# One-core attention and two feed-forward stages: SP's order of stores and loads in the second unit loop and at the start of the last stage

## The chip, the core and the metric

The kernel runs on one core of one Trainium2 chip. The metric is device time in microseconds (us) of the whole program. Three runs of the kernel before took 1477.15, 1477.49 and 1480.37 us; the median is 1477.49. Engines are named as in the profile: PE is TensorE, PEld its weight load, DVE VectorE, ACT ScalarE, POOL GpSimd, SP the engine whose queue issues nearly all DMAs.

## The reference

```python
def reference(**kwargs):                     # names cut
    attn_out = _attn_ref(q, k, v)            # keys and values mean-pooled by 8, softmax attention, 8 x 8 heads, 576 rows
    x = attn_out.transpose(0, 2, 1, 3).reshape(B * S, H * D)          # 4608 tokens x 512
    # stage 1: each token goes to one of 8 experts (argmax of gate logits + a bias by modality)
    #   h = max(x[mask] @ w1[e], 0);  out[mask] = gate_w * (h @ w2[e])          512 -> 1024 -> 512
    x = _moe_ref(x=x, **moe_kwargs)
    # stage 2, all tokens:  h = x @ w_in;  g = h * clip(h + 3, 0, 6) / 6;  g @ w_out   512 -> 2048 -> 512
    return _moe2_ref(x=x, **moe2_kwargs)
```

`w_in` and `w_out` come as float64, of which the kernel makes pairs of float32 (a high part and a rest).

## The kernel before, in words

Attention fills the first 210 us or so. Its end sorts the tokens by expert into a DRAM table `xr`, and a small table in SBUF (`tab`) says for each *unit* of 400 rows which expert it belongs to.

Stage 1 (`moe1`) works unit by unit (`unit`, L930). A unit has eight *steps* f, one per 128 hidden columns. In step f SP loads the weights of step f+3 into one of two buffers `ws`; ScalarE and VectorE split the weights of step f+2 into `wh` and `wl` (L783, L784); TensorE forms the hidden product `ph` (L942, 12 matmuls), then the output products `y` of step f-1 (L955, 12 matmuls). At the end of a unit the next unit's rows `cxg` are transposed (L868), where ScalarE also copies the token numbers out (`tkr`, L873), and `yo` takes the result, which the next unit stores to `yd`. There are one first unit, a loop of eight units (in each of which 1/8 of `w_in` is converted), a second loop whose count `n_l` is read from `nun` at run time (L1045), and a last unit.

The second loop (L1046, body at L1019 to L1031) converts three tiles of `w_out` in each pass. Each tile is loaded to `ds` (two buffers, L1306), goes through nine operations of ScalarE and VectorE (`f64_split`, L792 to L807) into `wv` (two buffers), and is stored to `vd` (L1031). The tiles are loaded in steps 0, 1 and 2. The operations stand in one list, from which each step takes four. The stores stand at the end of steps 3, 5 and 7.

Stage 2 (`moe2`) takes blocks of 768 tokens; each block is eight *quads* of seven products `hps` (L1118, six matmuls each, with operands `sq` loaded from `sd` into seven buffers, L1295), and in quad q the twelve groups of output products `ops` (L1108) of quad q-1 stand between them. In the first block VectorE and ScalarE also convert the rest of `w_out`, two operations at a time. The results go out by an indirect DMA whose row numbers are `tki`.

Each engine executes its own instructions in the order in which the Python code issues them (a manual schedule on PE, ACT, DVE and SP). An instruction that waits holds everything behind it on its engine. So where a store or a load stands among SP's instructions decides what its wait holds up.

```python
                cs[f] = g.wo_load(cd, f)                                  # L1021, steps 0, 1, 2
                if f > 0 and f % 2 == 1 and f // 2 in range(1, KD + 1):   # the store, steps 3, 5, 7
    nc.sync.dma_start(tkf, tok_d[0:NT].rearrange("(c p) -> p c", p=P))    # L1189
    while g.s_ahead < 7:
        g.s_load()
```

Of the kernel before, what the change touches and what calls it, by code (L numbers as in the profile page):

```python
# [8 lines left out]
F32 = mybir.dt.float32  # L9
F32R = mybir.dt.float32r  # L10
BF16 = mybir.dt.bfloat16
I32 = mybir.dt.int32
# [7 lines left out]
P = 128  # L20
# [4 lines left out]
NT = B * S  # L25
# [16 lines left out]
KD = 3  # L42
# [768 lines left out]
def moe1(tc, g, xr_d, tok_d, y_d, s_d, v_d, w1, w2, w_in):  # L811
    nc = tc.nc
# [109 lines left out]
    def conv_out(t):  # L922
        a, m, ex = (s.cv.tile([P, 4, P], I32, name=n, tag=n).rearrange("p k f -> p (k f)") for n in ("a", "m", "ex"))
        o = s.cv.tile([P, 2, DM], F32R, name="wv", tag="wv", bufs=2)
        return o, f64_split(nc, g, t[:, :, 1], t[:, :, 0], a, m, ex, o[:, 0], o[:, 1])
# [4 lines left out]
    def unit(i, first=False, last=False, tail=None, quad=None):  # L930
# [3 lines left out]
        cs = {}  # L934
# [15 lines left out]
        def y_mm(f):  # L950
            j = f % 4
            hi, lo = hh.pop(f)
            for d in range(4):
                for n, (a, b) in enumerate(((s.wh, hi), (s.wl, hi), (s.wh, lo))):
                    nc.tensor.matmul(yps[d], a[j][:, 1, d * P:(d + 1) * P], b, start=(f == 0 and n == 0), stop=(f == 7 and n == 2))  # L955

        lx = LX if first else 1
        parts = {LX: (0, 1, 2, 3)} if first else {1: (0,), 2: (1,), 3: (2,), 4: (3,)}
        ops = []
        for f in range(8):  # L960
            if first and f == 0:
                w_dma(e, 2)
            if f == lx and not last:
                en = reg(0, i + 1, E - 1)
            if f < 5 or not last:
                w_dma(e if f < 5 else en, (f + 3) % 8)
            if f == 0 and not first:
                col = reg(2, i, NT)
                if not last:
                    cc = quad  # L970
                    if quad is None:
                        cd = nc.values_load(g.tab[0:1, 3, bass.ds(i, 1)], engines=(ET.SP,), min_val=0, max_val=1)
            if f < 6 or not last:
                w_split((f + 2) % 8)
            h_mm(f)
            if f == lx and not last:
                rx = reg(1, i + 1, E * R - NW)
            if f in parts and not last:
                load_x(rx, parts[f])
            if f - 1 in parts and not last:  # L980
                gate_x(parts[f - 1])
            if f == 2:
                store_tok(0 if first else reg(2, i + 1, NT))
            if f == 3 and not first:
                store_y(col)
            if f == 7 and not last:
                for c in range(2):
                    transp(c, ps())
            if f > 0:
                y_mm(f - 1)  # L990
            if tail and next(tail, None):
                open3()
            if last:
                if f in (1, 2):
                    g.y_load(0, f - 1)
                if f == 3:
                    ops = g.y_ops(0)
                if f >= 3:
                    g.s_load()
                    for _ in range(3):  # L1000
                        if ops:
                            ops.pop(0)()
                if f >= 6:
                    g.wo_load(KD + NQ * (f - 6))
            elif quad is not None:
                if f == 0:
                    cs[0], cs[1] = conv_load(cc, 0), conv_load(cc, 1)
                if f == 1:
                    co, ops = conv(cs.pop(0))
                if f == 4:  # L1010
                    c1_, ops = conv(cs.pop(1))
                for _ in range(5):
                    if ops:
                        ops.pop(0)()
                if f == 4:
                    conv_store(co, cc, 0)
                if f == 7:
                    conv_store(c1_, cc, 1)
            elif not first:  # L1019
                if f < KD:  # L1020
                    cs[f] = g.wo_load(cd, f)  # L1021
                if 1 <= f <= KD:
                    co, o_ = conv_out(cs.pop(f - 1))
                    ops += o_
                    cs[8 + f] = co
                for _ in range(4):
                    if ops:
                        ops.pop(0)()
                if f > 0 and f % 2 == 1 and f // 2 in range(1, KD + 1):
                    n = f // 2  # L1030
                    nc.sync.dma_start(v_d[bass.ds(cd, 1), n - 1].rearrange("o p x -> p (o x)"),  # L1031
                                      cs.pop(8 + n).bitcast(F32).rearrange("p w f -> p (w f)"))
        if not last:
            for c in range(2, 4):
                transp(c, ps())
        y_mm(7)
        for d in range(4):
            (nc.scalar.copy if d % 2 else nc.vector.tensor_copy)(s.yo[:, d], yps[d])

    def run(tail):  # L1040
        open_ps()
        unit(0, first=True, tail=tail)
        with tc.For_i(0, NQ, 1, iteration_sync="reg_based") as i:
            unit(i + 1, quad=i)
        n_l = nc.values_load(g.nun, min_val=2, max_val=10)  # L1045
        with tc.For_i(0, n_l, 1, iteration_sync="reg_based") as i:  # L1046
            unit(i + NQ + 1)
        unit(n_l + NQ + 1, last=True)
        store_y(reg(2, n_l + NQ + 2, NT))
        es_p.close()  # L1050
        es_l.close()
        es_r.close()
# [3 lines left out]
    return c  # L1056


def moe2(tc, g, tok_d, v_d, out):


    nc = tc.nc
# [20 lines left out]
    def wo_get(f):  # L1083
        nc.sync.dma_start(wo[f].bitcast(F32).rearrange("p w f -> p (w f)"), v_d[f // NQ, f % NQ])

    tkf = c1.tile([P, NT // P], F32, name="tkf")
    tki = c1.tile([P, NT // P], I32, name="tki")
    pso = {}

    def put(j, t):  # L1090
# [95 lines left out]
        rest(6)  # L1186
        return [lambda fh=fh, th=th, t=t: o_group(j, q, fh, th, t, out_[fh, th]) for fh, th in ((0, 0), (1, 0), (1, 1), (0, 1)) for t in range(TC)]

    nc.sync.dma_start(tkf, tok_d[0:NT].rearrange("(c p) -> p c", p=P))  # L1189
    while g.s_ahead < 7:  # L1190
        g.s_load()
    wo_get(0)
# [3 lines left out]
    for n, f in enumerate(fs):  # L1196
        o_ = []
        cops += [lambda f=f, o_=o_: (o_.extend(conv(f)), o_.pop(0)())] + [lambda o_=o_: o_.pop(0)()] * 5
        if n + 2 < len(fs):
            cops.append(lambda f=fs[n + 2], o_=o_: (o_.pop(0)(), g.wo_load(f)))  # L1200
        cops += [lambda o_=o_: o_.pop(0)()] * (9 - len(cops) % 9 if len(cops) % 9 else 0)
    groups = []
    yo = []
    for j in range(NP):
        for q in range(NQ):
            extra = {i: [] for i in range(7)}
            if j == 0:
                for i in range(7):
                    for _ in range(2):
                        if cops:  # L1210
                            extra[i].append(cops.pop(0))
                if q == 1:
                    extra[0].append(lambda: v.tensor_copy(tki, tkf))
                if q < KD - 1:
                    extra[3].append(lambda q=q: wo_get(q + 1))
                    extra[4].append(lambda q=q: wo_get(NQ + q + 1))
# [24 lines left out]
def chunk_kernel(ctx, tc, q, k, v, mid, w_gate, mbias, w1, w2, w_in, w_out, out):  # L1241
# [9 lines left out]
    with tc.manual_schedule(engines={ET.PE, ET.Activation, ET.DVE, ET.SP}):  # L1251
# [5 lines left out]
            g.sp, g.yp = pool("ds"), pool("dy")  # L1257

        g.open_d = open_d
        g.raw, g.yc = {}, {}  # L1260
        g.sq, g.s_ahead = [], 0

# [49 lines left out]
        tail = attention(tc, g, c, (q, k, v, mid, w_gate, mbias), xr_d)  # L1312
        next(tail)
        c.run(tail)
        moe2(tc, g, tok_d, v_d, out)


# [28 lines left out]
```

## Time and profile before

| | |
|---|---|
| median of 3 runs | 1477.49 us (1477.15 to 1480.37) |
| profiled execution | 1480.39 us, span 1478.6 us |
| mean granted clock of PE | 0.973 |
| PE busy | 1400.0 us (95% of the span), 7673 matmuls |
| DVE busy | 948.0 us (64%) |
| ACT busy | 622.8 us (42%) |
| passes of the second loop | 2 (six stores `vd<-wv`) |

All views are of one profiled execution. Times in a view are us from the start of the span. [...] A stretch's busy time counts what an engine did in it; its length less that is standing. Waits of SP's queue and of the engines are listed apart.

### The profile page before, as it was taken

To read this page: it belongs to the slowest core of one execution; us is meant where nothing else is said; L and a number is where in the kernel's file an instruction comes from. 1 tells how busy PE (TensorE), PEld (TensorE's weight loads), DVE (VectorE), ACT (ScalarE), POOL (GpSimd) and SP (SyncE) were. 2 spreads that over 40 slices of the span, in tenths; PEclk is the share of its full clock that TensorE was granted. 3 is DMA by queue.
4 is the path that set the end of the run, shared out by engine and by line. 5 is a ranking of instruction groups with operands and counts; after the bars stand their busy time and mean duration, and the time that the engine had idled before them with its cause. 6 is when DMAs were issued, how large, how long until landed. Compare 5 with 4: busy or idle time off the path is not lost.

```text
span 1478.6 us, 24692 instructions
## 1 busy us (share of the span) xinstructions
PE 1400.0 (95%) x7673; PEld 1282.2 (87%) x7673; DVE 948.0 (64%) x1920; ACT 622.8 (42%) x1255; POOL 204.1 (14%) x231
## 2 busy tenths in 40 slices
PE   7998988999999999878899999999999999999998
PEld 6787877999999998878788888888888888888886
DVE  7899774778887876656687544644554465465443
ACT  3565653445555543444344333433333343333322
POOL 5555233111111111000000100000010000001001
PEclk8999998999999999999899999999999999999999
DMA  9974154777777766656754454454355445435441
GB/s 267 312 227 167 73 163 126 247 233 245 240 238 244 241 217 203 202 178 182 266 171 143 149 162 117 117 174 139 116 154 163 116 124 179 125 115 155 116 118 67
DMA packets 236172, 258.40 MB, mean 175 GB/s; under 512 B 25442, under 2 KB 197474, under 8 KB 236082
## 3 DMA queue, kind: packets, MB, share of 16 engines
q1 hardware_dynamic: 228882, 237.08, 53.0%
q0 software_dynamic: 7200, 20.18, 3.7%
q8 instruction: 49, 0.80, 0.2%
q14 instruction: 41, 0.34, 0.1%
HBM read 209.36 MB, written 55.24 MB: 179 GB/s over the span
## 4 chain that ended last, share of the span: by engine, by line
issue 50%; PE 3%; POOL 2%; DMA 1%; DVE 0%; POOLq 0%; ACT 0%; SPq 0%; ACTq 0%
POOL out_dram L1097 2%; PE ph L942 1%; PE y L955 1%; DMA sq<-sd 1%; PE hps L1118 0%; POOLq L1341 0%; ACT r L1129 0%; DVE r L1130 0%; DVE c L1139 0%; DVE da L795 0%; DVE dm L797 0%; POOLq L1097 0%; DVE gl L1134 0%; SPq L1189 0%; DVE dex L796 0%
## 5 line engine op out<-in xcount | busy, mean ns | idle before, releaser
L1118 PE MATMUL hps<-yc,sq 128*128 128x384 f32 x2004 | 411.9, 340 | 14.7 <-DVE c L1139 7.3
L1118 PEld LDWEIGHTS hps<-yc,sq 128*128 128x128 f32 x2004 | 362.8, 189 | 51.6 <-DVE c L1139 13.0
L1108 PE MATMUL ops<-wo,gh 128*128 128x512 f32 x1152 | 362.3, 395 | 0.0
L1108 PEld LDWEIGHTS ops<-wo,gh 128*128 128x128 f32 x1152 | 212.9, 188 | 23.0
L1108 PE MATMUL ops<-wo,gl 128*128 128x512 f32 x576 | 228.4, 397 | 0.0
L1129 ACT ACTIVATE r<-c,three 128x384 f32<-128x384 f32 x144 | 88.8, 617 | 225.9 <-DVE c L1139 225.5
L784 DVE TENSOR_TENSOR wl<-ws,wh 128x512 fp32r<-128x512 f32 x192 | 131.7, 719 | 60.4 <-ACT wh L783 53.1
L783 ACT CAST wh<-ws 128x512 fp32r<-128x512 f32 x192 | 115.0, 619 | 92.5 <-DMA ws<-in_moe_w_dram 67.7
L1133 ACT CAST gh<-r 128x384 fp32r<-128x384 f32 x192 | 98.6, 513 | 123.5 <-DVE r L1130 122.8
L1097 POOL DMA_INDIRECT out_dram<-osb,tki x36 | 35.3, 981 | 804.9 <-ACT osb L1095 774.5
L942 PE MATMUL ph<-xhi,wh 128*128 128x400 f32 x384 | 133.6, 348 | 7.1 <-issue 3.4
L955 PE MATMUL y<-hi,wh 128*128 128x400 f32 x384 | 136.6, 356 | 2.6 <-ACT hi L946 2.5
L955 PE MATMUL y<-lo,wh 128*128 128x400 f32 x384 | 135.3, 352 | 1.8 <-DVE lo L947 1.8
L942 PE MATMUL ph<-xlo,wh 128*128 128x400 f32 x384 | 134.2, 349 | 0.0
L955 PE MATMUL y<-hi,wl 128*128 128x400 f32 x384 | 133.9, 349 | 0.0
L942 PE MATMUL ph<-xhi,wl 128*128 128x400 f32 x384 | 133.9, 349 | 0.0
L1108 PEld LDWEIGHTS ops<-wo,gl 128*128 128x128 f32 x576 | 108.0, 188 | 26.3
L1134 DVE TENSOR_TENSOR gl<-r,gh 128x384 fp32r<-128x384 f32 x192 | 106.4, 554 | 27.0 <-ACT gh L1133 23.2
L1130 DVE SCALAR_TENSOR_TENSOR r<-r,c 128x384 f32<-128x384 f32 x144 | 80.4, 558 | 57.7 <-ACT r L1129 55.8
L860 POOL TENSOR_TENSOR cxg<-cxg 100x512 f32<-100x512 f32 x48 | 57.7, 1206 | 355.5 <-PE ph L942 178.1
L1129 ACT ACTIVATE r<-hps,three 128x384 f32<-128x384 f32 x48 | 27.9, 581 | 136.7 <-PE hps L1118 136.6
L1130 DVE SCALAR_TENSOR_TENSOR r<-r,hps 128x384 f32<-128x384 f32 x48 | 26.6, 553 | 90.2 <-ACT r L1129 90.1
(231 smaller groups left out, 1979.8 us busy)
## 6 DMA issues: line engine op xcount, KB each, us to landing
sq<-sd SPq DMA_DIRECT2D x336, 256.0 KB, 2.8
ws<-in_moe_w_dram SPq DMA_DIRECT2D x192, 256.0 KB, 3.8
sd<-wq SPq DMA_DIRECT2D x16, 896.0 KB
cxg<-xr SPq DMA_DIRECT2D x44, 225.8 KB
yd<-yo SPq DMA_DIRECT2D x12, 800.0 KB, 6.5
yr<-yd SPq DMA_DIRECT2D x12, 768.0 KB, 4.3
kv<-in_k_dram SPq DMA_DIRECT2D x16, 512.0 KB, 7.5
kv<-in_v_dram SPq DMA_DIRECT2D x16, 512.0 KB, 9.8
```

Of the source, the lines that this page charges most:

```text
L783: nc.scalar.copy(hi, src)
L784: nc.vector.tensor_tensor(lo, src, hi.bitcast(F32), op=ALU.subtract)
L860: nc.gpsimd.tensor_tensor(s.xg[:, t, 0:DM].rearrange("p (h x) -> p h x", x=D), v, s.xg[:, t, GC:GC + 1].unsqueeze(2).to_broadcast([T4, H, ...
L942: nc.tensor.matmul(ph, a[j][:, 0, k * P:(k + 1) * P], b[k], start=(n == 0), stop=(n == 11))
L955: nc.tensor.matmul(yps[d], a[j][:, 1, d * P:(d + 1) * P], b, start=(f == 0 and n == 0), stop=(f == 7 and n == 2))
L1097: i_ = nc.gpsimd.indirect_dma_start(out=out, out_offset=bass.IndirectOffsetOnAxis(ap=tki[:, c:c + 1], axis=0), in_=o, in_offset=None).ins
L1108: nc.tensor.matmul(pso[t_], gt[a][:, t * P:(t + 1) * P], wo[f][:, b], start=(q == 0 and fh == th and n == 0), stop=(q == NQ - 1 and fh != ...
L1118: nc.tensor.matmul(ps, w[:, kk, a * P:(a + 1) * P], y[:, b, kk], start=(start and n == 0), stop=(n == 5), skip_group_check=True)
L1129: a_.activation(r, c, AF.Relu, bias=g.three)
L1130: v.scalar_tensor_tensor(r, r, 6.0, c, op0=ALU.min, op1=ALU.mult)
L1133: a_.copy(gh, r)
L1134: late.append(lambda: v.tensor_tensor(gl, r, gh.bitcast(F32), op=ALU.subtract))
```

## The change

In the second loop a tile is loaded in steps 0, 1 and 4, its operations are taken five a step from steps 1, 3 and 5 on, and it is stored in steps 4, 6 and after the last products. The last unit loads one `sq` tile in each step from step 1 on (before: from step 3 on), loads the token numbers in step 3 as 36 rows of 128, and in step 7 transposes them on PE and casts them to `tki` on DVE. The read of the loop count stands before the first loop. In stage 2 the load of the conversion after next stands seven operations later.

```diff
+        def v_store(t, k):
+            nc.sync.dma_start(v_d[bass.ds(cd, 1), k].rearrange("o p x -> p (o x)"), t.bitcast(F32).rearrange("p w f -> p (w f)"))
...
+                if f == 3:
+                    nc.sync.dma_start(g.tk, tok_d[0:NT].rearrange("(c p) -> c p", p=P))
+                if f == 7:
+                    pt = ps()
+                    nc.tensor.transpose(pt[:, 0:NT // P], g.tk, g.idn[0:NT // P, 0:NT // P])
+                    nc.vector.tensor_copy(g.tki, pt[:, 0:NT // P])
+                if f >= 1:
+                    g.s_load()
                 if f >= 3:
-                    g.s_load()
...
             elif not first:
-                if f < KD:
-                    cs[f] = g.wo_load(cd, f)
-                if 1 <= f <= KD:
-                    co, o_ = conv_out(cs.pop(f - 1))
+                if f in (0, 1, 4):
+                    k = min(f, KD - 1)
+                    cs[k] = g.wo_load(cd, k)
+                if f in (1, 3, 5):
+                    cs[8 + f // 2], o_ = conv_out(cs.pop(f // 2))
                     ops += o_
-                    cs[8 + f] = co
-                for _ in range(4):
+                for _ in range(5):
                     if ops:
                         ops.pop(0)()
-                if f > 0 and f % 2 == 1 and f // 2 in range(1, KD + 1):
-                    n = f // 2
-                    nc.sync.dma_start(v_d[bass.ds(cd, 1), n - 1].rearrange("o p x -> p (o x)"),
-                                      cs.pop(8 + n).bitcast(F32).rearrange("p w f -> p (w f)"))
+                if f in (4, 6):
+                    v_store(cs.pop(8 + f // 2 - 2), f // 2 - 2)
...
         y_mm(7)
+        if 10 in cs:
+            v_store(cs.pop(10), 2)
...
         unit(0, first=True, tail=tail)
+        n_l = nc.values_load(g.nun, min_val=2, max_val=10)
         with tc.For_i(0, NQ, 1, iteration_sync="reg_based") as i:
             unit(i + 1, quad=i)
-        n_l = nc.values_load(g.nun, min_val=2, max_val=10)
...
-    nc.sync.dma_start(tkf, tok_d[0:NT].rearrange("(c p) -> p c", p=P))
...
-        if n + 2 < len(fs):
-            cops.append(lambda f=fs[n + 2], o_=o_: (o_.pop(0)(), g.wo_load(f)))
-        cops += [lambda o_=o_: o_.pop(0)()] * (9 - len(cops) % 9 if len(cops) % 9 else 0)
+        cops += [lambda o_=o_: o_.pop(0)()] * 3
+    for n, f in enumerate(fs[2:]):
+        one = cops[9 * n + 13]
+        cops[9 * n + 13] = lambda f=f, one=one: (one(), g.wo_load(f))
```

SP in the second loop before, from the weight load of step 5 (`ws`, two DMAs each) over the store of the second tile (`vd<-wv`) to the weight load of step 6; ISA and REGISTER_ALU are register instructions:

```order
L879 ISA
L879 DMA ws_2139<-in_moe_w_dram 128x512
L1031 ISA
L1031 REGISTER_ALU
L1031 DMA vd<-wv 128x1024
L877 ISA
L877 DMA ws_2140<-in_moe_w_dram 128x4x128
L879 ISA
L879 DMA ws_2140<-in_moe_w_dram 128x512
```

The same place in the change, with steps 5 and 6 in a row:

```order
L879 ISA
L879 DMA ws_2141<-in_moe_w_dram 128x512
L877 ISA
L877 DMA ws_2142<-in_moe_w_dram 128x4x128
L879 ISA
L879 DMA ws_2142<-in_moe_w_dram 128x512
L958 ISA
L958 DMA vd<-wv 128x1024
```

The second tile's store has moved behind the weight load of step 6; that of the third stands behind the weight load of step 7, the body's last.

SP at the end of the last unit and the start of stage 2 before: the last store of `yd`, the token numbers, then operands `sq` and converted tiles `wo`:

```order
L896 REGISTER_ALU
L896 DMA yd<-yo 128x4x400
L1189 DMA tkf<-tokd 128x36x1
L1295 DMA sq<-sd 128x2x256 x2
L1084 DMA wo_4643<-vd 128x1024
L1084 DMA wo_4635<-vd 128x1024
L1295 DMA sq<-sd 128x2x256 x3
L1306 DMA ds<-in_moe_w_out_dram 128x1024
L1084 DMA wo_4642<-vd 128x1024
L1295 DMA sq<-sd 128x2x256
```

The same place in the change:

```order
L896 REGISTER_ALU
L896 DMA yd<-yo 128x4x400
L1094 DMA wo_4653<-vd 128x1024
L1094 DMA wo_4645<-vd 128x1024
L1304 DMA sq<-sd 128x2x256 x3
L1094 DMA wo_4652<-vd 128x1024
L1304 DMA sq<-sd 128x2x256
L1094 DMA wo_4644<-vd 128x1024
L1304 DMA sq<-sd 128x2x256 x2
L1315 DMA ds<-in_moe_w_out_dram 128x1024
```

The load of the token numbers and two `sq` loads are gone from here (they stand in the last unit), and the load `ds` has moved from ahead of the second pair of `wo` loads to behind it.

## Rows read from the trace of the kernel before

**Rows 1.** The page, part 1: busy time (share of the span) and instructions of each engine.

```profile
PE 1400.0 (95%) x7673; PEld 1282.2 (87%) x7673; DVE 948.0 (64%) x1920; ACT 622.8 (42%) x1255; POOL 204.1 (14%) x231
```

**Rows 2.** Waits of TensorE, 552 to 712 us: us in total, times, longest.

```profile
PE pt L868 <- ACT tkr L873: 7.6, 2, 5.4
PE hps L1118 <- DMA sq<-sd: 6.7, 2, 4.0
PE ph L942 <- issue: 3.4, 1, 3.4
PE ph L942 <- PEq L1341: 3.4, 1, 3.4
```

**Rows 3.** Stretches: length, busy of PE, PEld, DVE, ACT, POOL; PEclk, DMA share, GB/s.

```profile
256.43:297.01 40.58, 38.51 (x209) 37.55 (x210) 30.00 (x52) 18.72 (x35) 4.27 (x4) 0.97 0.77 237
333.74:370.18 36.44, 36.44 (x210) 36.34 (x210) 29.43 (x53) 19.11 (x35) 4.72 (x4) 1.00 0.80 243
557.07:560.48 3.41, 3.41 (x12) 3.38 (x11) 0.58 (x1) 0.57 (x2) 0.00 (x0) 0.50 0.52 153
556.16:605.53 49.37, 42.09 (x209) 39.32 (x210) 31.20 (x51) 18.58 (x36) 4.93 (x4) 0.90 0.59 185
605.53:648.49 42.96, 38.74 (x210) 36.94 (x209) 31.64 (x52) 19.37 (x37) 4.44 (x4) 0.97 0.66 212
651.90:688.42 36.52, 36.52 (x192) 36.51 (x193) 22.84 (x33) 16.63 (x28) 0.00 (x0) 0.95 0.62 203
688.42:704.91 16.49, 9.79 (x43) 8.70 (x42) 10.89 (x23) 6.88 (x13) 0.00 (x0) 0.76 0.81 206
704.91:710.67 5.76, 5.76 (x16) 5.18 (x17) 2.06 (x5) 1.35 (x3) 0.00 (x0) 0.50 1.05 393
```

**Rows 4.** Waits of SP's queue, 555 to 652 us.

```profile
SPq L1031 <- DVE wv L807: 31.4, 6, 9.9
...
SPq L1046 <- DMA vd<-wv: 1.8, 1, 1.8
```

**Rows 5.** Timeline, 588 to 604 us: start, us, engine, line, operation, [idle before].

```profile
589.46 0.35 SPq L1031 DMA_DIRECT2D vd<-wv  x1
...
597.65 1.29 DVE L784 TENSOR_TENSOR wl<-ws,wh 128x512 fp32r<-128x512 f32 x2 [3.00 <-issue]
```

**Rows 6.** Waits of all engines, 555 to 652 us.

```profile
ACT wh L783 <- DMA ws<-in_moe_w_dram: 21.1, 12, 3.7
...
ACT ex L792 <- DMA ds<-in_moe_w_out_dram: 2.6, 2, 1.4
```

**Rows 7.** Timeline, 684 to 722 us.

```profile
688.42 4.57 PE L1118 MATMUL hps<-yc,sq 128*128 128x384 f32 x24
...
689.63 0.45 SPq L1189 DMA_DIRECT2D tkf<-tokd  x1
...
690.13 5.80 SPq L1295 DMA_DIRECT2D sq<-sd  x2
...
694.19 0.55 DVE L1139 TENSOR_TENSOR ww<-s,hps 128x384 f32<-128x384 f32 x1
...
695.73 0.55 DVE L1139 TENSOR_TENSOR c<-ww,ops 128x384 f32<-128x384 f32 x1
...
698.00 2.26 PE L1118 MATMUL hps<-yc,sq 128*128 128x384 f32 x6 [3.96 <-DMA sq<-sd]
...
704.91 2.29 PE L1118 MATMUL hps<-yc,sq 128*128 128x384 f32 x6 [2.73 <-DMA sq<-sd]
```

**Rows 8.** DMA view, 684 to 712 us: packets and their sizes.

```profile
DMA packets 8412, 6.17 MB, mean 220 GB/s; under 512 B 4864, under 2 KB 7692, under 8 KB 8411
```

**Rows 9.** Line 1045, the loop count's read: ns min/median/max, starts.

```profile
L1045 PEldq TENSOR_LOAD <-nun x1: 491/491/491, 554.0 to 554.0; - x1
```

**Rows 10.** Waits of TensorE, 712 to 800 us.

```profile
PE hps L1118 <- DVE c L1139: 0.8, 1, 0.8
```

**Rows 11.** DMA view, 300 to 550 us: packets by queue.

```profile
q1 hardware_dynamic: 63088, 60.20, 77.8%
```

More of the change, by code (lines that the diff above doesn't have):

```diff
@@ L1056, in moe1, with moe2 @@
     return c
-def moe2(tc, g, tok_d, v_d, out):
+def moe2(tc, g, v_d, out):
     nc = tc.nc
@@ L1084, in wo_get @@
         nc.sync.dma_start(wo[f].bitcast(F32).rearrange("p w f -> p (w f)"), v_d[f // NQ, f % NQ])
-    tkf = c1.tile([P, NT // P], F32, name="tkf")
-    tki = c1.tile([P, NT // P], I32, name="tki")
+    tki = g.tki
     pso = {}
@@ L1211, in moe2 @@
                             extra[i].append(cops.pop(0))
-                if q == 1:
-                    extra[0].append(lambda: v.tensor_copy(tki, tkf))
                 if q < KD - 1:
@@ L1259, in chunk_kernel @@
         g.open_d = open_d
+        g.tk = g.cp.tile([NT // P, P], F32, name="tk")
+        g.tki = g.cp.tile([P, NT // P], I32, name="tki")
         g.raw, g.yc = {}, {}
@@ L1314, in chunk_kernel @@
         c.run(tail)
-        moe2(tc, g, tok_d, v_d, out)
+        moe2(tc, g, v_d, out)
 _INS = ["q", "k", "v", "moe_modality_id", "moe_w_gate", "moe_modality_bias", "moe_w1", "moe_w2", "moe2_w_in", "moe2_w_out"]
```

## The prediction

> **What bounds the kernel now.** I read the engine shares first, then the mean and waits of TensorE, then stretches cut at the first matmul of each unit. [...] The waits of TensorE between 552 and 712 us name the standing: 7.6 us for a transpose behind ScalarE's `tkr`, 6.7 us for `sq` loads, 3.4 us at each end of the second loop [rows 2]. That is the region that the diff edits.
>
> The stretches give the size [rows 3]. A pass of the first loop takes 36.44 us with TensorE busy throughout. The second loop runs two passes in this execution (the six stores `vd<-wv` are three a pass), and they take 49.37 and 42.96 us for the same 210 matmuls and transposes. So 12.9 and 6.5 us are lost inside them. VectorE does 31.64 us of work in the second pass against 29.43 in the first loop's pass: 2 us more, well below 36.4, so VectorE's load is not the reason. The queue of SP is: it waited 31.4 us for VectorE at L1031, the store of a converted tile [rows 4]. SP works in order, so the weight loads of the next steps stand behind that store. In the first pass the second store went out only at 589.46, when TensorE had reached the eighth step's products. ScalarE accordingly stood 21.1 us waiting for weights [rows 6]. VectorE's `wl` of the last step came at 597.65, after 3.00 us in which nothing that the profile shows held it [rows 5]. TensorE stood 5.4 us there.
>
> The third place is the start of the last stage. SP issues the token-number load (L1189) at 689.63, and the two `sq` issues behind it span 5.80 us [rows 7], where the load of the token numbers itself is 0.45. Of the 8412 packets in 684 to 712 us, 4864 are under 512 B [rows 8]: that load reads 4608 numbers of 4 B, one packet each. TensorE stood 3.96 and 2.73 us for `sq` in the first quad [rows 7], and its clock was 0.50 until 710.67 [rows 3].
>
> **The change, part by part.** All is counted against the profiled execution: 1480.39 us, span 1478.6. The median of the runs shown, 1477.49, is 2.9 us lower; I subtract the same sum from it.
>
> *Stores two steps later, third load in step 4, five operations a step.* The instructions stay the same: three loads, 27 operations, three stores a pass. A tile's nine operations now fill steps 1 and 2 (3 and 4, 5 and 6), and its store stands in step 4 (6, end), so it finds its data ready; the weight load behind it no longer waits. What bounds a pass then? The first loop has the same 24 splits and its own 22 operations, at most five a step, and runs without a gap. I take 36.44 plus 0.8 for the 2 us more of VectorE: 37.2, so 5.8 less in the second pass. Bounds: 36.4 if nothing is late (6.5 less); 40 if ScalarE, whose queue takes the third tile one step after its load, stands for it (3 less): the waits of that kind in rows are small, 2.6 us in two [rows 6].
>
> The first pass pays for first use. The first loop's own first pass took 40.58, 4.1 above the later ones [rows 3]. Here the half clock from 557.07 to 560.48, which follows the 3.43 us of standing at the entry, costs 1.7, and stays. I take 36.4 + 1.7 + 3.4 = 41.5, so 7.9 less. Bounds: 38.1 (11.2 less), and 46.4 if the 3.00 us stop of VectorE still reaches TensorE with its half clock behind it (3 less). Step 7 now has no conversion operations, so that stop meets a VectorE with less behind it; that is why I go near the first loop's row.
>
> *Exit.* At the end of the second loop all engines meet, and SP there waits 1.8 us for the last store to land [rows 4]. The third store now goes out as soon as step 6 is done and lands during step 7 and the last products. 1.8 less; bounds 0 and 2.3. The last unit ran a little at 0.50 [rows 3], behind that standing of 3.4: the mean clock of 0.95 over 36.52 us is 1.8 lost. With 1.6 of standing I count half of it: 0.9 less, bounds 0 and 1.7.
>
> *Loop count read earlier.* Each engine reads the count in about 0.5 us [rows 9]. Between the loops all engines have just met, so it is paid in full (0.5 less); ahead of the first loop TensorE still has products queued, so I count 0.2 more. Bounds 0 and 0.5 less.
>
> *Last unit.* Two `sq` loads come in steps 1 and 2, so all seven are issued before the stage ends; there SP's DMA queue is free enough (share 0.62 [rows 3]) that weights are not late. Token numbers come as 36 rows of 512 B, are transposed by one TensorE instruction and cast by VectorE in step 7: 0.1 more (a 100x100 transpose is 0.25, pipelined). If weights did slip, the 4.6 us that a step lasts (36.44 over eight) is the bound.
>
> *Start of the last stage.* The 4608 packets and the blocked issue go. Next late are VectorE's operations. The first 24 matmuls took 4.57 us at full clock, 0.19 each [rows 7], so the 42 of the quad need 8.0. The sixth product overwrites what `ww` (694.19, 0.55) reads, the seventh what `c` (695.73, 0.55) reads [rows 7]; so TensorE waits 0.7 and some 0.5, and the quad ends near 697.5: 9.1 us instead of 16.49, 7.4 less. The half clock over the 5.76 us behind it gives back 2.9. Against that stands VectorE's debt, since TensorE reaches the second quad while VectorE still has about 3 us of the first quad's operations: I count 1.2, and 0.7 for a chance of 0.4 that the small waits still cost 1.7 in clock. Sum: 8.4 less. Bounds: 4 (TensorE is only let go when VectorE is done, and half the clock loss stays) and 10.5.
>
> *The loads of the later conversions* leave SP seven operations later. SP waits at them before, but TensorE's longest wait between 712 and 800 us is 0.8, for VectorE [rows 10], so I count nothing. The `sq` loads that stood behind it were covered by seven buffers; the price, if the later load makes ScalarE wait in turn, is a wait of the same 0.8 kind a few times, 3 at most.
>
> Sum: 7.9 + 5.8 + 1.8 + 0.9 + 0.3 - 0.1 + 8.4 = 25.0 less. From 1480.39 that is 1455.4, from the median 1452.5. All bounds on the poor side add up to about 10 less (1467.5), on the good side to 32.7 less (1445).
>
> **The rivals.**
> *First use and VectorE take the place of the waits.* The first pass keeps its 5.4 us gap and the clock behind it, since the 3.00 us stop is no SP wait, and the last stage gets only its lower bound of 4. For it: that stop and the debt are in rows. Against: in the second pass the same place cost 2.2 with weights late, and VectorE is freer now. 3 + 5.8 + 1.8 + 0.3 + 4 = 14.9 less: 1462.6.
>
> *The second loop stays bound.* If ScalarE and VectorE hand tiles to each other too late even with weights on time, the passes keep 49 and 43, and only the exit and the last stage gain: 1.8 + 0.3 + 8.4 = 10.5 less, 1467. Against it stands the first loop's pass with nearly the same load.
>
> *Slower: code is fetched in every pass.* The code before and in the loops moves in memory. [...] Against it: between 300 and 550 us every one of the 63088 packets is on the data queue, none on an instruction queue [rows 11]. [...]
>
> **How the numbers follow.** The forecast gets 0.73 (own range 1446 to 1459), the first rival 0.16, the second 0.07, the third 0.03, and 0.01 stays for no change. The range 1445 to 1467 takes in all bounds and the first two rivals. About 0.2% (3 us) is what a measurement of this kernel tells from no change. Faster: 0.73 + 0.16 + 0.07 = 0.96; same 0.01; slower 0.03.
>
> **What would show it.** Right: SP's waits at the stores all but gone; ScalarE's 21.1 us for weights down to a few; the second pass near 37 and the first near 41.5; the standing at the exit near 1.6; no packets of 4 B at the stage's start; the first quad near 9 us, with `DVE` named in place of `sq`. Wrong: a new wait of ScalarE for the third tile, an `issue` stop in every pass, or TensorE at 0.50 through the second quad.

## The result, and the profile after

The kernel after takes 1455.84 us (median of 4 runs, 1451.69 to 1457.83), the kernel before on the same chip 1478.93: ratio 0.984, 95% interval 0.9812 to 0.9868. The forecast was 1452.5 with a range of 1445 to 1467. The profiled execution is the fastest of the four, 1451.69 us with a span of 1450.0, so it is 28.7 us below the profiled one of before while the medians are 23.1 apart. So the terms of the sum are read from stretches and not from the total.

TensorE's share in the page (as in [rows 1]):

```profile
PE 1385.0 (96%) x7674; PEld 1269.4 (88%) x7674; DVE 948.3 (65%) x1920; ACT 623.1 (43%) x1255; POOL 204.5 (14%) x231
```

VectorE and ScalarE work as long as before; TensorE is busy 15 us less with the same matmuls and one transpose more, because fewer of them ran at a granted clock of 0.50 (mean granted clock 0.985 for 0.973) and, as will be seen, because many of them run slightly faster. The stretches of after, columns as in [rows 3]: a pass of the first loop, the second loop's two passes, its exit, the last unit, the first two quads, and all that follows.

```profile
371.36:407.78 36.42, 36.42 (x210) 36.32 (x210) 29.22 (x53) 19.11 (x35) 4.34 (x4) 1.00 0.79 243
556.55:600.52 43.97, 39.95 (x210) 37.34 (x211) 31.88 (x51) 18.87 (x36) 5.15 (x4) 0.96 0.71 222
600.52:637.10 36.58, 36.58 (x210) 36.15 (x209) 31.71 (x52) 19.56 (x37) 5.84 (x4) 1.00 0.72 231
637.10:638.28 1.18, 0.01 (x2) 0.04 (x1) 0.14 (x1) 0.53 (x2) 0.00 (x0) 1.00 0.00 0
638.28:674.28 36.00, 35.82 (x193) 34.91 (x194) 22.84 (x34) 16.34 (x28) 0.00 (x0) 1.00 0.67 222
674.28:684.10 9.82, 8.29 (x44) 7.03 (x43) 6.91 (x15) 4.30 (x9) 0.00 (x0) 1.00 0.85 292
684.10:700.32 16.22, 16.05 (x79) 14.02 (x79) 13.21 (x27) 6.56 (x13) 0.00 (x0) 1.00 0.99 340
700.32:1449.95 749.63, 733.78 (x3625) 653.75 (x3624) 406.24 (x728) 269.71 (x486) 35.38 (x36) 1.00 0.46 139
```

The last of them in the kernel before:

```profile
723.68:1478.64 754.96, 739.82 (x3624) 656.69 (x3624) 406.39 (x728) 269.67 (x486) 35.31 (x36) 1.00 0.46 138
```

The second pass has TensorE busy from end to end; the first quad has lost its half clock and most of its standing. The last stretch is 5.3 us shorter although nothing in it seems to have changed: the matmul counts differ by one record, the granted clock is the same, and neither has a long wait. The prediction had no term for that.

The waits of SP's queue, 553 to 645 us: the 31.4 us at the store [rows 4] are 5.2 (the store is now L958); the wait for the last store to land (L1056) is still 1.8, but now 3.9 for `yo`, the unit's result, come behind it, so the store no longer ends the loop. SP now waits at the weight loads instead, until `wl` is split and a buffer `ws` is free: 15.3 us (first line below), for 1.2 before (second fence). ScalarE's wait for weights, 553 to 640, is 14.0 for 21.1 [rows 6]; 11.6 of it fall into the first pass (553 to 600).

```profile
SPq L877 <- DVE wl L784: 15.3, 8, 2.7
SPq L958 <- DVE wv L807: 5.2, 2, 3.1
SPq L1056 <- DVE yo L1048: 3.9, 1, 3.9
...
SPq L1056 <- DMA vd<-wv: 1.8, 1, 1.8
```

```profile
SPq L877 <- DVE wl L784: 1.2, 3, 0.4
```

```profile
ACT wh L783 <- DMA ws<-in_moe_w_dram: 14.0, 10, 3.3
...
ACT ex L792 <- DMA ds<-in_moe_w_out_dram: 3.4, 2, 2.1
```

What is left of TensorE's waits, 553 to 698 us (before: [rows 2]):

```profile
PE ph L942 <- issue: 2.7, 1, 2.7
PE pt L868 <- ACT tkr L873: 2.1, 1, 2.1
PE ph L942 <- PEq L1350: 1.2, 1, 1.2
...
PE hps L1127 <- DVE ww L1148: 0.7, 1, 0.7
PE hps L1127 <- DMA sq<-sd: 0.6, 1, 0.6
```

The 0.7 for `ww` is the wait that the prediction named as next late. The packets of 4 B are gone (668 to 698 us; before 4864 under 512 B, [rows 8]):

```profile
DMA packets 4591, 7.64 MB, mean 255 GB/s; under 512 B 306, under 2 KB 3634, under 8 KB 4589
```

In the second loop's first pass, the one that stays long, SP issues nothing from 561.1 to 565.7 (its timeline), and nothing in the waits explains it:

```profile
560.76 0.34 SPq L1315 DMA_DIRECT2D ds<-in_moe_w_out_dram  x1
565.68 0.40 SPq L877 DMA_DIRECT2D ws<-in_moe_w_dram  x1
```

The DMA view of that pass holds packets on an instruction queue (first fence), that of the second pass none (second fence):

```profile
q1 hardware_dynamic: 7912, 9.71, 70.7%
q14 instruction: 3, 0.02, 0.2%
q8 instruction: 1, 0.02, 0.2%
```

```profile
q1 hardware_dynamic: 6520, 8.46, 72.3%
```

Near its end VectorE and ScalarE are late (timelines, 589 to 596 us):

```profile
589.73 0.68 DVE L797 SCALAR_TENSOR_TENSOR m<-ds,ex 128x512 f32<-128x512 uint32 x1
591.56 0.69 DVE L806 TENSOR_TENSOR ex<-a,wv 128x512 f32<-128x512 f32 x1 [1.15 <-ACT xhi L783]
592.28 0.69 DVE L807 TENSOR_TENSOR wv<-ex,m 128x512 fp32r<-128x512 f32 x1
592.89 1.28 DVE L784 TENSOR_TENSOR wl<-ws,wh 128x512 fp32r<-128x512 f32 x2
594.10 0.56 DVE L947 SCALAR_TENSOR_TENSOR lo<-ph,hi 128x400 fp32r<-128x400 f32 x1
594.58 0.56 DVE L784 TENSOR_TENSOR xlo<-pt,xhi 128x400 fp32r<-128x400 f32 x1
```

```profile
595.23 0.23 ACT L873 COPY tkr<-pt 4x100 f32<-4x100 f32 x1 [3.81 <-DVE xlo L784]
```

The third tile's last two operations and the last weights' split stand ahead of `xlo`; `tkr` waits 3.81 us for it, TensorE 2.10 us for `tkr`, and from 596.14 on its clock is 0.50 for 3.4 us.

VectorE has also stood itself: nothing runs there from 590.41 to 591.56. The profile names ScalarE's `xhi` for it, which L806 does not read. In the traces of the experiments with this loop (e1, e8, e9, e10, e12) VectorE stands at the same L806 for 0.92 to 2.52 us, and in e9 and e10 the profile finds nothing that it waits for (first fence: e10). In before it stood 3.00 us in the same part of the pass [rows 5]. One packet on an instruction queue falls close to the stop (second fence: DMA view of after, 589.2 to 592 us):

```profile
596.01 0.69 DVE L806 TENSOR_TENSOR ex<-a,wv 128x512 f32<-128x512 f32 x1 [2.52 <-issue]
```

```profile
q1 hardware_dynamic: 706, 0.61, 67.1%
q14 instruction: 1, 0.01, 1.1%
```

### The profile page after: what moved, and what is told of

Its sections match the earlier page's. It is cut to its first block, busy times and chain, and to the rows that moved or that the text cites. A ratio compares the mean times of both kernels' runs of the same rounds, so it can differ in the third digit from the quotient of the medians.

```text
span 1450.0 us, 24678 instructions
## 1 busy us (share of the span) xinstructions
PE 1385.0 (96%) x7674; PEld 1269.4 (88%) x7674; DVE 948.3 (65%) x1920; ACT 623.1 (43%) x1255; POOL 204.5 (14%) x231
## 4 chain that ended last, share of the span: by engine, by line
issue 51%; POOL 2%; PE 1%; DMA 1%; DVE 0%; POOLq 0%; ACT 0%; SPq 0%; DVEq 0%; ACTq 0%
POOL out_dram L1106 2%; DMA ws<-in_moe_w_dram 1%; PE ph L942 0%; PE y L955 0%; DVE t L1283 0%; DVE wl L784 0%; POOLq L1350 0%; ACT wh L783 0%; DVE yc L784 0%; DVE lo L947 0%; POOLq L1106 0%; SPq L877 0%; SPq L1304 0%; DVE tki L1006 0%; PE pt L1005 0%
## 5 line engine op out<-in xcount | busy, mean ns | idle before, releaser
L1127 PE MATMUL hps<-yc,sq 128*128 128x384 f32 x2004 | 405.8, 337 | 10.1 <-DVE c L1148 7.5
L1127 PEld LDWEIGHTS hps<-yc,sq 128*128 128x128 f32 x2004 | 357.6, 188 | 46.5 <-DVE c L1148 13.7
L1117 PE MATMUL ops<-wo,gh 128*128 128x512 f32 x1152 | 358.5, 392 | 0.0
L1117 PEld LDWEIGHTS ops<-wo,gh 128*128 128x128 f32 x1152 | 211.4, 188 | 23.1
L784 DVE TENSOR_TENSOR wl<-ws,wh 128x512 fp32r<-128x512 f32 x192 | 134.5, 737 | 51.3 <-ACT wh L783 42.1
L1117 PEld LDWEIGHTS ops<-wo,gl 128*128 128x128 f32 x576 | 107.9, 187 | 23.1
```

The source lines that it names most:

```text
L784: nc.vector.tensor_tensor(lo, src, hi.bitcast(F32), op=ALU.subtract)
L1117: nc.tensor.matmul(pso[t_], gt[a][:, t * P:(t + 1) * P], wo[f][:, b], start=(q == 0 and fh == th and n == 0), stop=(q == NQ - 1 and fh != ...
L1127: nc.tensor.matmul(ps, w[:, kk, a * P:(a + 1) * P], y[:, b, kk], start=(start and n == 0), stop=(n == 5), skip_group_check=True)
```

## The experiments

All ratios are to the kernel before in runs on the same chip. Its median was 1480.86 with the first four, 1480.69 with the next four, 1480.62 and 1478.51 with the two pairs. A "pass" is the stretch between the first matmuls of two units, so a second pass holds the exit too.

**The second loop alone (e1_loop2).** Before, with this part of the diff, here in short:

```
+ if f in (0, 1, 4):  load      + if f in (1, 3, 5):  conversion begins
- for _ in range(4):            + for _ in range(5):
- store in steps 3, 5, 7        + store in steps 4, 6 and after y_mm(7)
```

> The kernel before with the second-loop edits alone: loads in steps 0, 1 and 4, conversions begun in steps 1, 3 and 5, five operations a step, stores in steps 4, 6 and behind the last products. Loop count, last unit and last stage as before. My theory: the traces of before and after give 49.37 to 43.97 (5.4) in pass one, 42.96 to 36.58 (6.4) in pass two, about 1.8 at the exit, 0.5 in the last unit: 14.1 less, about 1465 us against 1479. Pass one still loses about 7 against pass two, since that loss is first use and not the stores. Rival one, the loop needs the earlier count as well (the entry then shows no half clock): pass one stays near 46 and the kernel at 1467 or more. Rival two, the steady quads of the last stage (15.82 to 15.69 us in the pair of traces) come from this edit: they would read 15.7 here and the kernel 1460.

Measured 1466.45, ratio 0.9903 (0.9884 to 0.9922): 14.4 less. The first pass took 45.32, the second with exit 37.78 (before 46.37), the last unit 35.07; quads 15.8 again. Rival two did not hold. Rival one cannot be told from the theory here: the pass and the time lie between the two, and the entry shows a half clock; but e9 and e10, which read the count early, take 47.3 and 46.3 for this pass, so the early read is not what it lacks. First pass, first quad, and the rest behind the second quad:

```profile
556.23:601.55 45.32, 41.17 (x209) 39.17 (x210) 32.09 (x51) 18.70 (x36) 4.91 (x4) 0.92 0.69 215
...
674.40:689.70 15.30, 9.80 (x44) 8.71 (x43) 10.02 (x21) 6.34 (x12) 0.00 (x0) 0.79 0.82 206
...
707.73:1463.02 755.29, 740.08 (x3624) 656.63 (x3624) 406.42 (x728) 269.63 (x486) 35.28 (x36) 1.00 0.46 138
```

**The last unit and the stage's start alone (e2_front).** Before, with these lines:

```
+ if f >= 1: g.s_load()
+ if f == 3: dma_start(g.tk, tok_d as 36 rows)     + if f == 7: transpose, cast to g.tki
- tkf, tki in pool "dc"; dma_start(tkf, tok_d in words of 4 B); tensor_copy(tki, tkf)
```

> The kernel before with the edits of the last unit and the last stage's start alone: token numbers as 36 rows, transposed and cast in step 7, sq loads from step 1, no 4-byte load, no tkf and tki in the last stage's memory. Second loop as before. My theory: first quad 16.49 to 9.8 and second 18.8 to 16.2, 9.3 less, about 1469.6 against 1479; later quads as before (15.8). Rival one, the memory that the two tiles no longer take moves the operands of the last stage and this is why the later quads read 15.69 in the trace of after: then another 5 less, 1464.5. Rival two, the stage start only gains when the second loop's exit leaves the clock at 1.00 in the last unit: then the first quad stays near 12 and the kernel at 1473.

Measured 1470.8, ratio 0.9928 (0.9906 to 0.9949): 10.1 less. But not as expected: the first quad is 9.74, the second stayed at 19.55 (18.77 before), so the start gave 6.0 in this trace, not 9.3; the rest is 749.69 and gave 5.3. Here TensorE waits 2.9 us for VectorE's `c` in the second quad. With the second loop mended too, that quad takes 16.22; why `c` is late in the one and not in the other is not shown.

```profile
696.17:705.91 9.74, 8.30 (x43) 7.04 (x42) 6.83 (x15) 4.28 (x8) 0.00 (x0) 1.00 0.85 292
705.91:725.46 19.55, 16.45 (x78) 13.83 (x78) 13.27 (x28) 6.51 (x12) 0.00 (x0) 1.00 0.77 274
725.46:1475.15 749.69, 733.80 (x3624) 653.81 (x3624) 406.33 (x728) 269.76 (x486) 35.38 (x36) 1.00 0.46 139
```

**The token numbers alone (e3_tok),** as e2_front with `g.s_load()` left in steps 3 to 7.

> The kernel before with the token numbers alone changed (36 rows in the last unit, no 4-byte load at the stage's start); five of the seven sq loads still come in the last unit and two at the stage's start. My theory, that the 4608 packets and the issue that they block are the cost: the two sq loads now issue in about 0.5 us each at 690 and land before TensorE asks for the sixth, so nearly all of the 9.3 is there, 8 less, 1471. Rival, that two sq loads at the stage's start are late whatever stands before them: first quad 12 to 13, about 4 less, 1475.

Measured 1471.64, ratio 0.9935 (0.9917 to 0.9954): 9.2 less. The total is near the theory's, the place is not: the first quad is 11.51 (a wait of 2.0 for `sq`), the second 19.21, so the start gave 4.5, near the 4 of the rival, and again 5.3 came from behind the second quad (749.66).

**The `sq` loads alone (e4_sq),** as e2_front's first line, with the 4-byte load kept.

> The kernel before with the sq loads alone moved (all seven in the last unit, from step 1); the 4-byte load of the token numbers stays at the stage's start. My theory: the first quad has its seven operands and ends after 9 to 10 us, but the blocked issue (about 6 us) now stands ahead of the next stage loads, so the second quad waits for its first sq: of the 9.3 some 5 are there, 1474. Rival one, only the missing operands mattered and the blocked queue is hidden behind seven buffers: 9 less, 1470. Rival two, the packets themselves hold the DMA queues so long that TensorE stands as long as before, one quad later: 0 to 2 less, 1477 to 1479.

Measured 1477.42, ratio 0.9971 (0.9958 to 0.9984): 3.4 less, between the theory and rival two. First quad 12.17, second 18.53, the rest 755.02. SP's timeline shows the price of the 4-byte load moved on to the `wo` loads behind it, as 5.80 in [rows 7] at the `sq` loads:

```profile
694.21 0.45 SPq L1190 DMA_DIRECT2D tkf<-tokd  x1
694.71 5.78 SPq L1085 DMA_DIRECT2D wo<-vd  x2
```

So both edits are needed for the first quad's 9.8, and the tokens' edit alone carries the 5.3.

**Stores alone, and loads alone (e5_stores, e6_loads).** In the second loop of before:

```
e5:  store in steps 5, 7 and after y_mm(7)      (loads in 0, 1, 2; four operations a step)
e6:  loads in 0, 1, 4; conversions from 1, 3, 5; five operations a step      (stores in 3, 5, 7)
```

> The kernel before with the three stores of a second-loop pass alone moved two steps later (steps 5, 7 and behind the last products); loads stay in steps 0, 1, 2, conversions from step 1, four operations a step. My theory, that SP standing at the stores is the whole loss of the later pass: pass two near 37 to 38, exit about 1.8 less, pass one 45 to 46, so 12 less, 1469 against 1481. Rival, that the third load, which must wait in step 2 for the first tile's buffer, holds SP in the stores' place: it waits there for two steps of VectorE, pass two near 40, pass one near 48, 5 less, 1476.

> The kernel before with the loads and operations of the second loop alone changed (loads in steps 0, 1 and 4, conversions from steps 1, 3 and 5, five operations a step); the stores stay in steps 3, 5 and 7, so each stands one step behind the step in which its tile is finished. My theory, that the distance of the store decides and one step is too little since SP issues about two steps ahead of VectorE: SP still waits some 10 to 15 us there, passes 47 and 40, 5 less, 1476 against 1481. Rival, that nine operations in two steps are enough wherever the store stands: passes 45 and 37, 10 to 12 less, 1469, and the exit stays at 3.4.

Measured: e5 1474.11, ratio 0.9956 (0.9942 to 0.997), 6.6 less; passes 48.27 and 41.25. e6 1469.72, ratio 0.9931 (0.9917 to 0.9944), 11.0 less; passes 47.54 and 40.04. In e5 the times are near those of its rival, but not for its reason: the third load's wait is 1.8, and the stores still wait 15.8. In e6 the rival has the total, the second pass and the exit right; only the first pass is as long as in the theory. The waits of SP's queue, 555 to 650 us, in e5 (first fence) and e6:

```profile
SPq L958 <- DVE wv L807: 15.8, 2, 9.2
...
SPq L1309 <- DVE m L797: 1.8, 2, 1.2
```

```profile
SPq L1031 <- DVE wv L807: 9.5, 5, 3.0
```

In e5 the third tile is still worked four operations a step, and its store waits. With one step between tile and store (e6) SP still waits a little at five of six stores. With both, 5.2 is left. But SP's wait and the pass are two things. Here is e6's second pass, without the exit, and the exit:

```profile
602.45:639.27 36.82, 36.82 (x210) 36.27 (x208) 31.95 (x51) 19.79 (x37) 4.73 (x4) 1.00 0.71 222
639.27:642.48 3.21, 0.00 (x1) 0.03 (x1) 0.14 (x1) 0.52 (x2) 0.00 (x0) 1.00 0.01 3
```

The loads and the denser operations alone keep TensorE busy through the whole second pass, with the stores where they were. In e5 the exit is 1.2 and the second pass without it about 40.1. So the operations set the second pass, and the later store sets the exit.

**Where the 5.3 us come from (e8_shift, e10_layout, e11_transpose).** In the traces of before, after and e1 to e4 the stretch behind the second quad took 749.6 to 749.7 or 755.0 to 755.3, and only kernels with the token edit had the first. The median spacing of two products of one width shows it, in after for before: 0.174 us for 0.176 (384 columns) and 0.231 for 0.233 (512).

```
e8:   g.cp.tile([P, 8], F32)                                    after; first pool, 32 B
e10:  c1.tile([P, 36], F32); c1.tile([P, 36], I32)              after; pool "dc" behind the wo tiles, 320 B
e11:  nc.tensor.transpose(ps()[:, 0:36], g.idn[0:36, :], ...)   before; step 7 of the last unit
```

> The kernel after with one unused tile of 32 bytes a partition more in the first memory pool, so that all tiles of the last stage stand 32 bytes higher; no instruction changes. In before, and in the two runs with before's memory, the operands of the last stage begin 32 bytes behind a multiple of 64 and the stage behind its second quad takes 755.0 us; in after, and in the two runs with the token tiles moved, they begin at multiples of 64 and it takes 749.7. My theory, that this is the 5.3 us which the prediction's sum did not hold: the part behind the second quad goes back to 755, the kernel to 1461 against 1455.8. Rival, that the removed 4-byte load or the missing cast gave it: 749.7 stays and the kernel reads 1455.8.

> The kernel after with two unused tiles of the sizes of tkf and tki (160 bytes a partition each) allocated again behind the wo tiles of the last stage; no instruction changes. What the run of e8_shift left open is why every quad takes 15.69 us where the token edit is made and 15.82 where it is not. Theory, the distance between tiles: in before the tiles gh and gl (TensorE's weights in the second product) stand 320 bytes farther from wo, sq and yc than in after. Then the part behind the second quad goes from 749.7 back to 755.0 here, and the kernel from 1455.8 to 1461. Rival, an instruction of the token edit (the transpose on TensorE in the last unit, or the cast and the load that went): 749.7 and 1455.8 stay.

> The kernel before with one more transpose on TensorE in step 7 of the last unit, of 36 rows of the identity, with a result that nothing reads; the token numbers, memory and all else as before. The other half of the question of e10_layout. If the one instruction more (a weight load and a product, so that all that follows stands one pair later) sets the pace of the last stage: the part behind the second quad takes 749.7 instead of 755.0, and the kernel is 5 less, 1475.5 against 1480.8. If the distance between tiles sets it: 755.0 stays and the kernel is within 0.3 of 1480.8.

e8: 1453.59, ratio 0.982 (0.9802 to 0.9837): alignment to 64 bytes fell. e10: 1459.98, ratio 0.985 (0.9823 to 0.9877): the stretch is back at 754.94, with every instruction as in after. e11: 1480.2, ratio 0.9996 (0.9983 to 1.0009), stretch 754.96: the extra transpose is not it. The stretch in e8 (first fence) and e10:

```profile
702.06:1451.75 749.69, 733.82 (x3625) 653.84 (x3624) 406.36 (x728) 269.71 (x486) 35.29 (x36) 1.00 0.46 139
```

```profile
705.40:1460.34 754.94, 739.76 (x3625) 656.87 (x3624) 406.37 (x728) 269.60 (x486) 35.27 (x36) 1.00 0.46 138
```

So where tiles stand in SBUF sets 5.3 us: the change moved `tkf` and `tki` out of pool "dc", and `gh`, `gl` and all tiles behind them came 320 bytes nearer to `wo`, `sq` and `yc`. All four layouts fit the distance between the tiles, since e8 moves all of them together; but its shift is only 32 bytes, so the place of `gh`, `gl` and the rest by itself is not ruled out. Which tiles it is, and why, the runs don't tell: `yc` and `sq`, the operands of `hps`, stand ahead of pool "dc" and do not move in e10, and yet the spacing of these products (384 columns) changes too.

**The first stage's operands (e9_align1, e12_distance).** Both are after with unused bytes in pool c1; e12 also spaces `xhi`, `xlo`, `hi`, `lo`:

```
e9:   p.tile([P, 8], F32)  at the end of c1
e12:  p.tile([P, 16], F32) ahead of xhi;  xhi, xlo, hi, lo: p.tile([P, 448], F32R)[:, 0:NW]
```

> The kernel after with one unused tile of 32 bytes a partition more at the end of the pool c1 (right side), so that the operands of the first stage's products (xhi, xlo, wh, wl, hi, lo), which begin 32 bytes behind a multiple of 64 in before and after, begin at multiples of 64. If the start of an operand costs TensorE here what it does in the last stage (0.8% of 36.4 us a pass): passes of the first loop near 36.1, 12 units x 0.3 = 3.5 less, 1452.3 against 1455.8. Rival, that only operands of the last stage's shapes (256 and 512 columns) feel it, and 400-column operands do not: passes stay at 36.42 and the kernel at 1455.8.

> The kernel after with the operands of the first stage's products set at one distance from each other: xhi, xlo, hi and lo take 1792 bytes a partition instead of 1600 (400 columns of it used) and 64 bytes lie ahead of them, so that wh, wl, xhi, xlo, hi and lo all stand at the same place modulo 256 bytes; in after they stand at many. No instruction changes. [...] Rival, that 256 bytes is not the measure, or that only the last stage feels it: passes 36.4, the kernel 1455.8.

e9: 1456.28, ratio 0.9835 (0.9819 to 0.9852), passes 36.4 to 36.6: its rival held. e12: 1453.6, ratio 0.9828 (0.9814 to 0.9842). Its passes are 36.11 for 36.42, the same count of matmuls at full clock, which its rival's 36.4 does not fit. An estimate from the spacings comes near it: at the pace of the last stage in after, 0.231 us for 512 columns, 400 columns would take 0.180 for the median of 0.182 here, about 0.3 over the 192 products of a pass.

```profile
369.16:405.27 36.11, 36.11 (x210) 36.03 (x210) 29.04 (x53) 18.94 (x35) 4.57 (x4) 1.00 0.78 245
```

That is some 2.5 us over the first loop's eight units, but the kernel's own time can't be told from after's by these intervals: the second loop's first pass took 46.66 in this trace, the last unit 38.05.

**The long first pass (e13_twoops).** After, with two operations for nine in `conv_out`:

```
- f64_split(...)        nine operations into wv
+ [tensor_scalar(o[:, w], t[:, :, w], 3, 0x3FFFFFFF, shift, and) for w in range(2)]
```

> The kernel after with two of the nine operations of each conversion in the second loop (two of VectorE; five more of VectorE and two of ScalarE are left out, so the converted values are not those of the reference); loads and stores stay. What it tells apart is why the loop's first pass takes 44 to 47 us where its second takes 36.6. My theory, first use of the loop's code: SP stands about 4 us at the pass's start whatever is computed, so weights come late and TensorE stands and loses clock: pass one still 42 to 45, second pass with exit 37.6. Rival, that the conversions' operations stand between VectorE and the weights' splits, and that the pass would make the late start good without them: pass one 38 to 40, the kernel 5 to 6 less, 1450 against 1455.8.

Measured 1448.85, ratio 0.9792 (0.9777 to 0.9807), some 7 below after (0.9792 against 0.984, of 1478.5): nearer to the rival than to the theory, though the pass, 40.98, is a little above the rival's 38 to 40.

```profile
557.00:597.98 40.98, 38.90 (x209) 37.77 (x210) 20.11 (x36) 15.12 (x30) 4.65 (x4) 0.96 0.74 233
```

SP stands as long as in after at this place (561.6 to 566.3 us in its timeline), and the pass still loses 4.4 against 36.6; of these, 2.3 are TensorE busy longer (38.90 for 36.58), with the half clock at the entry that after does not have. The other 3 to 6 us of the full kernel go when the seven operations go, which stand ahead of the late weights' splits and `xlo`. The wait for `tkr` and the half clock behind it are absent. But VectorE's stop is absent too, and so is the packet on the instruction queue (DMA view, 567 to 597.9 us), so this run does not tell the operations' own time from the stop:

```profile
q1 hardware_dynamic: 6982, 8.41, 87.1%
```

## Why the prediction was right, point by point

The terms, as far as the pair of traces shows them: second pass 6.4 less (predicted 5.8); exit 2.2 (1.8); last unit 0.5 (0.9); entry 0.8 (the loop count's 0.3); start of the last stage 9.2 (8.4); first pass 5.4 (7.9). These make 24.5 against 25.0 predicted. Outside the sum: 5.3 less behind the second quad, 1.5 and 0.3 less in the first loop's first two passes, 3.0 more ahead of the loops. The last three are the spread between executions: over all traces here the first loop began at 255.5 to 260.6 us and its first pass took 39.1 to 42.1, whatever the kernel. Together this is the 28.7 between the profiled executions, within 0.1.

*The second pass* was right in size, and weights that come in time are what it gains by. But the prediction gave this to stores that find their data ready, and e6 shows that they need not: with the loads and five operations a step alone the pass takes 36.82, while SP still waits 9.5 us at the stores. The later stores alone (e5) leave about 40.1.

*The exit* came out with its reason, and e5 (1.2) against e6 (3.21) shows that the store's place is it: the third store goes out at 630.51 in the timeline, before the last products, and SP waits for `yo` last. TensorE stands 1.18 for 3.41.

*The first pass* is the term that was mis-sized. "36.4 + 1.7 + 3.4" took the first loop's first pass for what first use costs. e13 gives nearly that number, 40.98, but only with two of nine operations. With all of them it is 43.97 here and 45.3 to 47.3 in the five other traces with this loop (before's loop: 49.4 to 51.3), so about 4.5 less by the means, 45.9 for 50.4. The step that failed is "Step 7 now has no conversion operations, so that stop meets a VectorE with less behind it": the third tile's last two operations (0.69 us each) reach VectorE behind the stop all the same, when it is late, and stand ahead of the last weights' split and `xlo`. So stop and operations together still reach TensorE, as 2.1 us in after and 3.7 and 3.9 in e9 and e10, with a half clock behind it. That is the prediction's own poor case: the mean of 45.9 is near its bound of 46.4. What the stop and the operations cost each is not shown, since e13 lacks both. The half clock at the entry did not simply stay either. It is absent in the traces of after and e8 and present in those of e9, e10, e12 and e13, all with 2.6 us of standing.

*The start of the last stage* had its mechanism: the packets and the blocked issue went, `ww` was next late at 0.7. e2 shows what the sum hid: alone the edit gives 6.0, with VectorE late for the second quad in that trace. e1 alone gives 1.9, and together they gave 9.2.

*ScalarE's wait for weights* was to go down to a few; it is 14.0, most of it in the first pass, the one that stays long.

*The later conversion loads* at nothing: the stretch behind the second quad is 749.6 with them (after) and without (e2, e3). *The loop count* was not tried alone; with the late read (e1) the entry's pass is 39.89, with the early one 39.2 (after, e8, e10).

*The rivals.* The first (first use and VectorE take the place) had the right suspects for the pass: a wait for `tkr` and a half clock remain there, at 2.1 for 5.4 us (3.7 and 3.9 in e9 and e10); in the last stage it did not hold. The second loop is no longer bound by the handing of tiles (36.58). Code fetched in each pass fell: of the second loop's passes in after the first holds four packets on instruction queues, and the second none, its 6520 packets being all on the data queue. No run here shows that a fetch stops an engine, or what one costs.

*The bounds.* The poor side, "about 10 less", leaves out two bounds that the prediction gives itself, 4.6 for the last unit and 3 for the later loads. With them it would be 2.4 less, 1475, outside the stated range.

By the medians 23.1 were gained for 25.0 predicted; e8 and e9, which run the same instructions, gained 27.1 and 24.4 on their chip. Of that some 5 is the place of the tiles, which nobody asked for; e10, which is without it, gained 20.6, 4.4 short of the forecast and still in its range. So the time was right with two errors of opposite sign in it, the first pass and the place of the tiles, and that they offset each other in part is luck.

## What to carry to other kernels

SP waited 31.4 us at stores whose data was not done, with the weight loads behind them, and 5.2 in after: such a store belongs behind the step in which its data is surely done, and the work that it stores must be dense enough to be done by then. Try the halves apart: later stores alone gave 6.6 us, denser work alone 11.0, both together 14.4, and waits of SP's queue of at most 3.0 us each (e6) cost the second pass nothing. The second loop's first pass took 43.97 us for the second's 36.58, and 40.98 with two operations for nine (e13): it had no slack, so work that the later pass hid stood on the path there. Look at what is queued ahead of the late splits, and at an engine's stops that no wait explains, before pricing such a pass from another loop. A diff that drops or moves a tile can move the tiles behind it (here by 320 bytes, worth 5.3 us); when a stretch with the same instructions changes pace, put unused bytes back before explaining it by the edit.

## What the runs showed of the hardware

- 320 bytes more between `wo` and the tiles behind it took the last stage behind its second quad from 749.63 us (after) to 754.94 (e10), about 0.7%, at a granted clock of 1.00 in both. The median spacing of two products of one width was 0.231 us in after and 0.233 in before (512 columns), 0.174 and 0.176 (384). A shift of all tiles by 32 bytes changed nothing (e8: 749.69), nor did one of the first stage's operands together (e9: passes of 36.4 to 36.6 us). With the operands of the first stage spaced to one place modulo 256 bytes a pass took 36.11 us for 36.42 (e12).
- At a granted clock of 0.50 the 400-column products of the second loop's entry started 0.333 us apart (before, 557.2 to 560.2 us), at 1.00 they start 0.182 apart (the first loop's median).
- After a standing of 2.6 us at the second loop's entry the granted clock fell in some executions (0.66 from 559.25 to 562.25 us in e9, 0.50 from 560.30 to 563.30 in e10) and stayed at 1.00 in others (after, e8), with the same instructions.
- In the first pass of the second loop SP issues nothing for 4.6 to 5.2 us at the same place in all fourteen traces (4.58 in after, 5.10 in before), and in the six with the new loop and all its operations VectorE stands 0.9 to 2.5 us at L806. In after packets on instruction queues fall close to both, two from 560.5 to 566 us and one from 589.2 to 592; its second pass has no such packet.
- Behind the read of 4608 numbers of 4 B SP's next two issues took 5.8 us, wherever it stood, ahead of the `sq` or of the `wo` loads ([rows 7], e4); without it the two `sq` issues took 1.59 (e3). The read's own issue took 0.45.
